# Nine token slots one chunk earlier, the fourth chunk turned on TensorE, three half slots made whole, and one table for the order of all queues

## The chip, the cores and the metric

The kernel runs on one core of a Trainium2 chip. The metric is the device time of one execution in microseconds, median of the runs. Engines: TensorE (PE, matmuls), VectorE (DVE), ScalarE (ACT), GpSimd (POOL, which issues the scatters and the stores) and SyncE (SP, which issues most loads and all turning DMAs).

## The reference

Two stages. A gated linear recurrence runs over 4 sequences of 5056 steps and 256 features, and its output, 20,224 tokens of 256 features, goes through a mixture of 8 experts, where each token takes its best one:

```python
a_t = np.exp(8.0 * sigmoid(r_gate) * log(a_base))
x_gated = np.sqrt(np.maximum(1.0 - a_t * a_t, 1e-06)) * sigmoid(i_gate) * x
h = a_t[:, t] * h + x_gated[:, t]          # for every step t; y[:, t] = h
logits = x @ w_gate                        # x is y, as 20224 x 256
e_idx = np.argmax(logits, axis=1)
h = np.maximum(x[mask] @ w1[e], 0.0)       # 256 -> 1024
out[mask] = gate_w * sigmoid(x @ w_output_gate)[e] * (h @ w2[e])
```

## The kernel before

**Chunks.** The 158 tiles of 128 tokens are worked in 21 chunks: two of four tiles (0 and 1), then chunks of eight, each in blocks of four tiles (512 tokens). Features lie on the partitions, so the recurrence is a scan along the row. For each block `chunk(c)` (L725) loads the gates and x (L752, on SP's queue), makes the gates on ACT (L758, L761, L768, L772, L777) and DVE (L764, L780) and scans on DVE (L812, last column kept by L815). Then the states are *turned*, so that tokens lie on partitions, and *routed*: logits, argmax (L1035 to L1047), a token's rank among those of its expert (matmuls `pk`, L1053 and L1055), its row (L1086 to L1093). GpSimd scatters each tile's rows (L545) to the DRAM array `xs`, which has one region for each expert.

There are two ways of turning. Chunks under `BY_PE` (0 and 1) are turned by TensorE: `project` (L932) multiplies the states, in fp32, by the identity and the two gates, so that turned states and logits come out of PSUM together; ACT writes the high half of the turned states (L948), DVE copies the logits (L951) and writes the low half (L952). All other chunks are split first (ACT the high part, L972; DVE the low part, L979, behind a memset, L977) into `rt`; a turning DMA on SP's queue (L988, the *flip*, one for each block) brings them to `rows_all`, while PE makes the logits from the split states (L996) and DVE sums them (L1004).

**Slots.** `slot(s)` (L1203) runs one expert's network on 128 rows (later 256) of its region. It fetches on SP's queue the address (L1223), the rows by a turning DMA (L1234) and each row's weight and token number (L1235). Layer 1 is L1306 on PE, in two halves of four 128-feature tiles: three f16 products for each weight. ACT takes the relu (L1331, high half), DVE the low half (L1334, `h`), layer 2 is L1381, ACT scales the result (L1402) and GpSimd stores it (L1405). The PSUM tile of layer 1 is free again when its low is done. Slots of the first set are *plain*: they work in fp32 with the weights as loaded (L1276, L1292, L1327, L1367).

`SETS` is the list of fixed slots: a tuple (chunk, first expert, last expert + 1, rows) says that after the counts of this chunk each of these experts has enough rows for one more slot. Each set costs five small DVE operations in `counts` (L1103 to L1112). So slots 0 to 7 need chunk 1, slots 8 to 15 chunk 3, slots 16 to 23 chunk 4, slots 24 to 31 chunk 5. What is left of the rows at the end goes to `ENDS` slots of 128 rows and `HALVES` slots of 64.

**Weights.** `unit(u)` loads one expert's w1 (u even) or w2 (u odd), finds its scale (a gram matrix of it on PE, L627; ACT L633; PE L636; DVE L641, L642) and splits it in two f16 parts (ACT L669, DVE L679). Units 14 and 15, expert 7 of the kernel's numbering, are staged in two pieces each (`fw14_0`, `fw14_1`, `fw15_0`, `fw15_1`) in buffers of the ring `hh`, which the hidden tiles `h` also use.

**The order.** Each step is a `Work` item of an engine or queue. `PLACES` holds a number for each as its rank; `in_order` (L188) runs them through a model of engines and queues and takes of those that are ready in the model the one with the least rank, so that the instructions stand in fixed order on PE, ACT and DVE, and on the DMA queues as they come:

```python
    for w, v in zip(first, places(len(first))):
        w.rank = v
        for w in in_order([w for w in works if not w.late], {"DVE": 1.7, "ACT": 0.8}):
            w.emit()
```

Of the kernel before, what the change touches and what calls it, by code (L numbers as in the profile page):

```python
# [7 lines left out]
F32 = mybir.dt.float32  # L8
# [17 lines left out]
SETS = [(1, 0, 8, 128), (3, 0, 8, 128), (4, 0, 8, 128), (5, 0, 8, 128), (6, 0, 8, 128), (8, 0, 8, 128), (9, 0, 8, 128), (10, 0, 8, 128),  # L26
        (12, 0, 8, 256), (14, 0, 8, 256), (16, 0, 8, 256), (18, 0, 8, 256), (20, 0, 8, 256)]
PROGRAM = "ccwwwwswswswssssws"
PLAIN = (0,)
# [4 lines left out]
BY_PE = 2  # L34
TOP = 6

ENDS = 16
HALVES = 3
# [290 lines left out]
def rglru_moe(ctx: ExitStack, tc: tile.TileContext, x, r_gate, i_gate, a_param, wg, wog, w1, w2, out, shape):  # L329
# [1155 lines left out]
    for w, v in zip(first, places(len(first))):  # L1485
        w.rank = v
# [48 lines left out]
```

## Time and profile before

| what | value |
|---|---|
| runs, median (lowest to highest) | 1009.37 us (1009.24 to 1009.7) |
| the profiled execution, its own time | 1010.89 us |
| its span, first to last instruction | 1009.0 us |
| mean granted TensorE clock | 0.977 |
| PE busy | 940.9 us, 93% of the span |
| DVE busy | 678.2 us, 67% |
| ACT busy | 624.1 us, 62% |
| POOL busy | 359.9 us, 36% |

Busy shares are means over the span. Two phases lie in it: up to about 680 us chunks are scanned and routed beside the slots, and DVE is busy most of the time; after that only slots run, and PE alone is full. The idle time of PE lies in the first quarter. A row of a timeline gives the start, the busy time, the line, the operation, how many instructions it sums up, and in brackets how long the engine had been idle before and what ended that. A start less the next start is what a group costs; busy times of neighbours overlap. A clock of 0.50 is 1.2 GHz, 1.00 is 2.4 GHz.

### The profile page before, as it was taken

To read this page: it belongs to the slowest core of one execution; us is meant where nothing else is said; L and a number is where in the kernel's file an instruction comes from. 1 tells how busy PE (TensorE), PEld (TensorE's weight loads), DVE (VectorE), ACT (ScalarE), POOL (GpSimd) and SP (SyncE) were. 2 spreads that over 40 slices of the span, in tenths; PEclk is the share of its full clock that TensorE was granted. 3 is DMA by queue.
4 is the path that set the end of the run, shared out by engine and by line. 5 is a ranking of instruction groups with operands and counts; after the bars stand their busy time and mean duration, and the time that the engine had idled before them with its cause. 6 is when DMAs were issued, how large, how long until landed. Compare 5 with 4: busy or idle time off the path is not lost.

```text
span 1009.0 us, 27629 instructions
## 1 busy us (share of the span) xinstructions
PE 940.9 (93%) x10796; PEld 860.5 (85%) x10796; DVE 678.2 (67%) x1719; ACT 624.1 (62%) x931; POOL 359.9 (36%) x341
## 2 busy tenths in 40 slices
PE   1389959999999999999999999999999999999996
PEld 1379859998999899999888888988888888899994
DVE  5789998888978898889878987878322222322231
ACT  8799987877777688877778777743322322322321
POOL 2115252544444444445344554444221211221111
PEclk9779988999999999999999999999999999999998
DMA  9999997989999999899988898656522122138771
GB/s 318 338 264 330 241 211 184 218 191 221 212 222 200 209 253 255 166 228 221 249 179 224 203 250 210 122 125 208 113 52 53 48 54 49 47 111 229 247 232 37
DMA packets 269237, 189.75 MB, mean 188 GB/s; under 512 B 211071, under 2 KB 222080, under 8 KB 269104
## 3 DMA queue, kind: packets, MB, share of 16 engines
q1 hardware_dynamic: 249488, 138.37, 59.5%
q0 software_dynamic: 15408, 42.22, 13.7%
q10 hardware_dynamic: 4208, 7.34, 2.0%
q8 instruction: 88, 1.44, 0.6%
q14 instruction: 45, 0.37, 0.1%
HBM read 79.09 MB, written 44.82 MB: 123 GB/s over the span
## 4 chain that ended last, share of the span: by engine, by line
PE 59%; DVE 13%; ACT 11%; DMA 10%; issue 4%; POOL 1%; SPq 1%; ACTq 0%; POOLq 0%; DVEq 0%
PE po L1381 27%; PE ph L1306 27%; DMA out_dram<-ot,osc 3%; DVE it L812 3%; DVE h L1334 3%; DMA it<-in_i_gate_dram 3%; PE po L1367 2%; DVE it L780 2%; ACT it L772 2%; ACT it L777 1%; ACT L777 1%; PE ph L1292 1%; DVE peak L864 1%; DVE xt L764 1%; DMA fw<-in_moe_w_dram 1%
## 5 line engine op out<-in xcount | busy, mean ns | idle before, releaser
L1381 PE MATMUL po<-w2r,h 128*128 128x256 f16 (+2 forms) x3720 | 494.5, 273 | 2.8 <-ACT ot L1402 1.3
L1306 PE MATMUL ph<-xt,w1r 128*128 128x128 f16 (+1 forms) x4608 | 427.1, 241 | 3.9 <-DMA xt<-xs 3.0
L1381 PEld LDWEIGHTS <-h 128*128 128x128 f16 (+1 forms) x3720 | 347.5, 98 | 41.9 <-issue 3.5
L1306 PEld LDWEIGHTS <-w1r 128*128 128x128 f16 x4608 | 349.2, 98 | 30.5 <-DMA xt<-xs 3.4
L1334 DVE SCALAR_TENSOR_TENSOR h<-ph,h 128x512 f16<-128x512 f32 (+1 forms) x310 | 208.3, 680 | 225.6 <-ACT h L1331 222.8
L1331 ACT ACTIVATE h<-ph 128x512 f16<-128x512 f32 (+1 forms) x310 | 180.6, 588 | 253.0 <-PE ph L1306 156.6
L1405 POOL DMA_INDIRECT out_dram<-ot,osc x163 | 174.9, 1073 | 424.7 <-ACT ot L1402 367.0
L545 POOL DMA_INDIRECT xs<-rows_all,posi x158 | 180.0, 1139 | 207.5 <-ACT h L1331 93.9
L1402 ACT ACTIVATE ot<-po,osc 128x256 f32<-128x256 f32 (+1 forms) x163 | 73.2, 469 | 62.2 <-PE po L1381 41.1
L812 DVE TENSOR_TENSOR_SCAN it<-rt,last,it 128x512 f32<-128x512 f32 (+4 forms) x78 | 96.1, 1241 | 0.5
L780 DVE SCALAR_TENSOR_TENSOR it<-it,xt 128x1024 f32<-128x1024 f32 (+1 forms) x40 | 48.3, 1208 | 28.9 <-ACT it L777 28.9
L768 ACT ACTIVATE rt<-rt,lam 128x512 f32<-128x512 f32 (+1 forms) x80 | 62.5, 803 | 2.4 <-issue 1.7
L1306 PE MATMUL ph<-xt,ws 128*128 128x128 f16 (+1 forms) x912 | 63.8, 215 | 0.0
L764 DVE SCALAR_TENSOR_TENSOR xt<-it,xt 128x1024 f32<-128x1024 f32 (+1 forms) x40 | 48.2, 1205 | 18.1 <-ACT it L761 18.1
L1306 PEld LDWEIGHTS <-ws 128*128 128x128 f16 x912 | 55.8, 98 | 4.1 <-issue 2.0
L761 ACT ACTIVATE it<-it 128x1024 f32<-128x1024 f32 (+1 forms) x40 | 41.5, 1040 | 16.1 <-DMA it<-in_i_gate_dram 16.1
L979 DVE SCALAR_TENSOR_TENSOR rt<-it,scale,rt 128x512 f16<-128x512 f32 (+1 forms) x76 | 48.9, 685 | 1.9 <-ACT rt L972 1.8
L772 ACT ACTIVATE it<-rt 128x1024 f32<-128x1024 f32 (+1 forms) x40 | 41.6, 1044 | 10.0 <-DVE xt L764 9.2
L758 ACT ACTIVATE rt<-rt 128x1024 f32<-128x1024 f32 (+1 forms) x40 | 41.7, 1043 | 9.3 <-DMA rt<-in_r_gate_dram 9.0
L777 ACT ACTIVATE it<-it,quarter 128x1024 f32<-128x1024 f32 (+1 forms) x40 | 44.8, 1134 | 0.3
L972 ACT ACTIVATE rt<-it,scale 128x1024 f16<-128x1024 f32 (+1 forms) x38 | 42.0, 1131 | 4.2 <-DVE scale L886 4.1
L864 DVE TENSOR_REDUCE peak<-it 128x1 f32<-128x1024 f32 (+1 forms) x34 | 40.0, 1193 | 0.0
(186 smaller groups left out, 694.1 us busy)
## 6 DMA issues: line engine op xcount, KB each, us to landing
rt<-in_r_gate_dram SPq DMA_DIRECT2D x39, 512.0 KB
it<-in_i_gate_dram SPq DMA_DIRECT2D x39, 512.0 KB
xt<-in_x_dram SPq DMA_DIRECT2D x39, 512.0 KB
ws<-w1r SPq DMA_DIRECT2D x38, 512.0 KB
w1r<-in_moe_w_dram ACTq DMA_DIRECT2D x4, 1024.0 KB
w2r<-in_moe_w_dram SPq DMA_DIRECT2D x4, 1024.0 KB
w2r<-in_moe_w_dram ACTq DMA_DIRECT2D x3, 1024.0 KB
w1r<-in_moe_w_dram SPq DMA_DIRECT2D x3, 1024.0 KB
```

The costliest lines, as they stand in the source:

```text
L545: op = nc.gpsimd.indirect_dma_start(out=xs[:, :], out_offset=bass.IndirectOffsetOnAxis(ap=pos, axis=0), in_=rows.bitcast(F32), in_offset=None,
L768: nc.scalar.activation(r[:, h], r[:, h], AF.Exp, scale=lam[:, h:h + 1], bias=lam[:, h:h + 1])
L772: nc.scalar.activation(t("it"), t("rt"), AF.Square)
L777: nc.scalar.activation(t("it"), t("it"), AF.Sqrt, scale=-0.25, bias=quarter)
L780: nc.vector.scalar_tensor_tensor(t("it"), t("it"), 0.5e-3, t("xt"), op0=ALU.max, op1=ALU.mult)
L812: nc.vector.tensor_tensor_scan(H[:, h, lo:hi], A[:, h, lo:hi], H[:, h, lo:hi], first, op0=ALU.mult, op1=ALU.add)
L1306: nc.tensor.matmul(ph[:, i, 0:w], lhsT=ws[:, f // 2 % 2, a, c, f % 2 * P:(f % 2 + 1) * P], rhs=xt[:, b * ND + c, 0:w], start=n == 0, stop= ...
L1331: newest["relu"] = nc.scalar.activation(part(0, f0), tiles["ph", s, f0][:, :, 0:w], AF.Relu).ins
L1334: nc.vector.scalar_tensor_tensor(part(1, f0), tiles["ph", s, f0][:, :, 0:w], 0.0, part(0, f0), op0=ALU.max, op1=ALU.subtract)
L1381: nc.tensor.matmul(po[0:pw, j], lhsT=hh[:, a, f % 4, j * P:j * P + pw], rhs=second(b), start=f + j + a + b == 0, stop=f == NF - 1 and a == ...
L1402: nc.scalar.activation(ot[0:pw], tiles["po", s][0:pw, j], AF.Copy, scale=tiles["osc", s][0:pw, j, 0:1])
L1405: op = nc.gpsimd.indirect_dma_start(out=out[:, :], out_offset=bass.IndirectOffsetOnAxis(ap=tiles["osc", s][0:pw, j, 1:2].bitcast(I32), axi ...
```

## The change

*Sets.* Experts 0 to 5 get their second slot after chunk 2 and no longer after chunk 3; of the slots that stood after chunk 4, those of experts 3 to 5 stand after chunk 3, beside the second slots of experts 6 and 7. So nine slots stand a chunk earlier. Slots 8 to 13 now need chunk 2, 14 to 18 chunk 3, 19 to 23 chunk 4; from 24 on nothing moves. There are three sets more.

*Turning.* Chunk 3 is turned by PE, like chunks 0 and 1: eight tiles of `project`, no flips, no logit matmuls.

*The end.* Nineteen slots of 128 rows in place of sixteen of 128 and three of 64.

*The order.* `in_order` and its ranks are no longer used for the main part; `ORDER` lists every work item, on all engines and queues, in the order in which it is emitted. `PLAIN` is a dictionary and the plain slots may have another width; both leave the eight plain slots as they are. In the changed file lines stand 5 earlier up to L1420 and 9 earlier near the end.

```diff
@@ -23,19 +23,19 @@
-SETS = [(1, 0, 8, 128), (3, 0, 8, 128), (4, 0, 8, 128), (5, 0, 8, 128), (6, 0, 8, 128), (8, 0, 8, 128), (9, 0, 8, 128), (10, 0, 8, 128),
+SETS = [(1, 0, 8, 128), (2, 0, 6, 128), (3, 6, 8, 128), (3, 3, 6, 128), (4, 0, 3, 128), (4, 6, 8, 128), (5, 0, 8, 128), (6, 0, 8, 128), (8, 0, 8, 128), (9, 0, 8, 128), (10, 0, 8, 128),
         (12, 0, 8, 256), (14, 0, 8, 256), (16, 0, 8, 256), (18, 0, 8, 256), (20, 0, 8, 256)]
...
-PLAIN = (0,)
+PLAIN = {0: 0}
...
-BY_PE = 2
+BY_PE = (0, 1, 3)
...
-ENDS = 16
-HALVES = 3
+ENDS = 19
+HALVES = 0
...
-PLACES = (
...
+ORDER = (
...
-def places(n):
+def laid_out(n):
...
-    return struct.unpack(f"<{n}H", zlib.decompress(base64.b85decode("".join(PLACES))))
+    return itertools.accumulate(struct.unpack(f"<{n}h", zlib.decompress(base64.b85decode("".join(ORDER)))))
...
-        for b in range(0, nt, 4) if c < BY_PE else ():
+        for b in range(0, nt, 4) if c in BY_PE else ():
...
-        if c >= BY_PE:
+        if c not in BY_PE:
             for blk, (pu, pold) in zip(blocks, pus):
...
-        plain = set_of[s] in PLAIN
+        plain = expert is not None and expert >= PLAIN.get(set_of[s], E)
...
-    first = [w for w in works if not w.late]
-    for w, v in zip(first, places(len(first))):
-        w.rank = v
-
     engines = {PE, mybir.EngineType.Activation, mybir.EngineType.DVE}
     with tc.manual_schedule(engines=engines):
-        for w in in_order([w for w in works if not w.late], {"DVE": 1.7, "ACT": 0.8}):
-            w.emit()
+        for k in laid_out(len([w for w in works if not w.late])):
+            works[k].emit()
```

On SP's queue, around the fetch of slot 8 (`xt16_8`) and the pieces of the last weights, before (the rows that only set up a fetch's address are left out):

```order
L752 DMA it_5_4_1509<-in_i_gate_dram 128x2x512
L988 DMA_TRANSPOSE rows_all_134<-rt_4_0_828 128x19x128
L1223 TENSOR_LOAD firsti_1_1325
L1234 DMA_TRANSPOSE xt16_8_1562<-xs_84 128x4x128
L1235 DMA mt_8_1563<-xs_84 128x2
L601 DMA fw15_1_1571<-in_moe_w2_dram 128x4x256
```

and after:

```order
L596 DMA fw14_0_1393<-in_moe_w1_dram 128x1024
L596 DMA fw14_1_1420<-in_moe_w1_dram 128x1024
L1218 TENSOR_LOAD firsti_1_994
L1229 DMA_TRANSPOSE xt16_8_1428<-xs_84 128x4x128
L1230 DMA mt_8_1429<-xs_84 128x2
L596 DMA fw15_0_1487<-in_moe_w2_dram 128x4x256
L596 DMA fw15_1_1531<-in_moe_w2_dram 128x4x256
```

Slot 8's fetch stands ahead of both pieces of `fw15`, and no flip of chunk 4 stands between them (the two flips follow after the fetches of slots 10 and 11).

On DVE, around the low half of slot 8's first hidden tile (`h_8_0`), before:

```order
L679 SCALAR_TENSOR_TENSOR w2r_136<-fw15_0_1476,wsc_137,w2r_136 128x1024
L679 SCALAR_TENSOR_TENSOR w2r_136<-fw15_1_1571,wsc_137,w2r_136 128x1024
L1086 TENSOR_TENSOR pos_4_1748<-pk_4_1712,carry_131 128x64
L1090 TENSOR_TENSOR pos_4_1748<-pos_4_1748,oh_4_1665 128x64
L1093 TENSOR_REDUCE posi_4_1751<-pos_4_1748 128x8
L1062 TENSOR_TENSOR df_4_1622<-oh_4_1665,lz_4_1582 128x64
L1063 TENSOR_REDUCE sm_4_1769<-ex_4_1639 128x8
L1064 TENSOR_REDUCE zs_4_1767<-df_4_1622 128x8
L1334 SCALAR_TENSOR_TENSOR h_8_0_1759<-ph_8_0_1612,h_8_0_1759 128x4x128
L780 SCALAR_TENSOR_TENSOR it_5_4_1509<-it_5_4_1509,xt_5_4_1358 128x1024
L1334 SCALAR_TENSOR_TENSOR h_8_1_1797<-ph_8_4_1632,h_8_1_1797 128x4x128
L1334 SCALAR_TENSOR_TENSOR h_9_0_1810<-ph_9_0_1699,h_9_0_1810 128x4x128
```

and after:

```order
L674 SCALAR_TENSOR_TENSOR w2r_133<-fw15_0_1487,wsc_134,w2r_133 128x1024
L674 SCALAR_TENSOR_TENSOR w2r_133<-fw15_1_1531,wsc_134,w2r_133 128x1024
L999 TENSOR_REDUCE lz_4_1692<-lg_4_0_1515 128x64
L1343 TENSOR_SCALAR osc_7_1702<-mt_7_1278 128x1
L1344 SCALAR_TENSOR_TENSOR osc_7_1702<-again_0_500,mt_7_1278 128x1
L999 TENSOR_REDUCE lz_4_1692<-lg_4_4_1629 128x64
L1030 TENSOR_REDUCE mx_4_1727<-lz_4_1692 128x8
L1031 TENSOR_TENSOR df_4_1729<-lz_4_1692,mx_4_1727 128x64
L1329 SCALAR_TENSOR_TENSOR h_8_0_1694<-ph_8_0_1517,h_8_0_1694 128x4x128
L759 SCALAR_TENSOR_TENSOR xt_5_4_1535<-it_5_4_1625,xt_5_4_1535 128x1024
L1329 SCALAR_TENSOR_TENSOR h_8_1_1741<-ph_8_4_1539,h_8_1_1741 128x4x128
L1329 SCALAR_TENSOR_TENSOR h_9_0_1750<-ph_9_0_1685,h_9_0_1750 128x4x128
```

The positions (`pos_4`, `posi_4`) and the sums (`sm_4`, `zs_4`) of chunk 4 no longer stand ahead of `h_8_0`, and of chunk 5 only the first product (L759) does, where before it was both of these, a scan pair and the first gated input (L775 now, L780 then).

## Rows read from the trace of the kernel before

**Rows 1.** Page part 1: busy time, share of the span, instructions.

```profile
PE 940.9 (93%) x10796; PEld 860.5 (85%) x10796; DVE 678.2 (67%) x1719; ACT 624.1 (62%) x931; POOL 359.9 (36%) x341
```

**Rows 2.** Windows around the hole: stretch, busy us by engine, granted clock, DMA.

```profile
130.00:140.00 10.00, 7.91 (x80) 7.24 (x78) 9.28 (x15) 9.89 (x13) 8.78 (x5) 1.00 0.97 248
140.00:145.00 5.00, 0.82 (x14) 0.61 (x14) 5.00 (x10) 4.66 (x6) 1.33 (x1) 0.82 0.67 157
145.00:155.00 10.00, 5.48 (x35) 4.81 (x36) 6.57 (x14) 5.82 (x9) 1.23 (x1) 0.50 0.90 141
155.00:160.00 5.00, 5.00 (x45) 4.34 (x44) 4.77 (x7) 4.81 (x5) 0.00 (x0) 0.81 1.04 275
```

**Rows 3.** PE's timeline: start, length, line, count, wait before it.

```profile
143.66 0.21 PE L996 MATMUL lg<-g,rt 128*128 128x32 bf16 x1 [3.95 <-DVE rt L979]
...
146.73 1.46 PE L1306 MATMUL ph<-xt,w1r 128*128 128x128 f16 x12 [1.81 <-DMA xt<-xs]
...
151.84 1.03 PE L627 MATMUL pg<-fw 128*128 128x128 bf16 x8 [2.79 <-DMA fw<-in_moe_w_dram]
...
240.47 1.18 PE L1306 MATMUL ph<-xt,w1r 128*128 128x128 f16 x18 [1.16 <-DMA xt<-xs]
```

**Rows 4.** Timeline of SP's DMA queue.

```profile
135.59 5.44 SPq L988 DMA_TRANSPOSE rows_all<-rt  x1
...
146.01 0.37 SPq L601 DMA_DIRECT2D fw<-in_moe_w_dram  x1
```

**Rows 5.** DVE's timeline at slot 8's first low and slot 22's second.

```profile
154.09 0.16 DVE L641 TENSOR_SCALAR wsq<-pg 128x1 int32<-128x1 int32 x1 [3.26 <-PE pg L636]
...
161.22 0.69 DVE L1334 SCALAR_TENSOR_TENSOR h<-ph,h 128x512 f16<-128x512 f32 x1 [0.53 <-ACT h L1331]
...
240.14 0.69 DVE L1334 SCALAR_TENSOR_TENSOR h<-ph,h 128x512 f16<-128x512 f32 x1 [0.46 <-ACT h L1331]
```

**Rows 6.** Windows behind the hole.

```profile
161.20:240.20 79.00, 76.76 (x1088) 71.88 (x1085) 69.21 (x179) 60.74 (x88) 37.41 (x33) 1.00 0.85 199
225.00:250.00 25.00, 22.58 (x320) 21.07 (x317) 21.43 (x59) 16.25 (x24) 11.62 (x10) 1.00 0.97 229
```

**Rows 7.** PE's timeline: starts of like groups in a row.

```profile
31.39 0.71 PE L932 MATMUL lg<-iw,it 128*128 128x144 f32 x4
31.93 0.65 PE L932 MATMUL prow<-iw,it 128*128 128x144 f32 x4
...
182.67 0.26 PE L996 MATMUL lg<-g,rt 128*128 128x48 bf16 x4
182.77 0.49 PE L1381 MATMUL po<-w2r,h 128*128 128x256 f16 x3
...
979.73 0.50 PE L1306 MATMUL ph<-xt,ws 128*128 128x128 f16 x6
980.07 0.49 PE L1381 MATMUL po<-w2r,h 128*128 x3
...
982.07 0.34 PE L1306 MATMUL ph<-xt,ws 128*128 128x64 f16 x6
982.24 0.82 PE L1381 MATMUL po<-w2r,h 128*128 x6
```

**Rows 8.** DVE's groups by line and shape: busy, mean ns of one, idle before.

```profile
L812 DVE TENSOR_TENSOR_SCAN it<-rt,last,it 128x512 f32<-128x512 f32 x70 | 88.6, 1275 | 0.5
L979 DVE SCALAR_TENSOR_TENSOR rt<-it,scale,rt 128x512 f16<-128x512 f32 x74 | 48.1, 691 | 1.9 <-ACT rt L972 1.8
...
L764 DVE SCALAR_TENSOR_TENSOR xt<-it,xt 128x1024 f32<-128x1024 f32 x39 | 47.5, 1218 | 18.1 <-ACT it L761 18.1
...
L952 DVE SCALAR_TENSOR_TENSOR rows_all<-prow,scale,rows_all 128x256 f16<-128x256 f32 x6 | 2.8, 473 | 0.0
...
L1103 DVE SCALAR_TENSOR_TENSOR first<-carry,next_row 128x8 f32<-128x8 f32 x13 | 2.2, 166 | 0.4
...
L951 DVE COPY lz<-prow 128x16 f32<-128x16 f32 x6 | 1.0, 164 | 0.2 <-ACT rows_all L948 0.2
```

More of the change, by code (lines that the diff above doesn't have):

```diff
@@ L744, in load @@
                 bufs = rings[tags[k]].n
-                wide_ = c >= BY_PE and tags[k] == PLANES
+                wide_ = c not in BY_PE and tags[k] == PLANES
                 t = pool.tile(
@@ L886, in level_of_peak @@
             nc.vector.tensor_scalar(sc, sc, float(254 + TOP << 23), None, op0=ALU.add)
[L888 removed]
+        if c not in BY_PE:
             pus = [rings["ps_r"].new() for _ in blocks]
@@ L901, in chunk @@
             en = work("PE", 0.25, energy, [mo], EARLY + c / 100, uses=[pu0], slack=SLACK[c > 4])
-            le = work("DVE", 0.3 + 0.15 * (c >= BY_PE), level, [en], late_rank, uses=[pu0])
+            le = work("DVE", 0.3 + 0.15 * (c not in BY_PE), level, [en], late_rank, uses=[pu0])
         else:
@@ L1038, in chances @@
         def chances():
-            nc.scalar.activation(st("ex", E), st("df", E), AF.Exp, scale=1.0 if c < BY_PE else tiles["inv_of", c])
+            nc.scalar.activation(st("ex", E), st("df", E), AF.Exp, scale=1.0 if c in BY_PE else tiles["inv_of", c])
         def chosen():
@@ L1066, in outer @@
         def outer():
-            nc.scalar.activation(st("zs", 1), st("zs", 1), AF.Exp, scale=-1.0 if c < BY_PE else tiles["inv_of", c])
+            nc.scalar.activation(st("zs", 1), st("zs", 1), AF.Exp, scale=-1.0 if c in BY_PE else tiles["inv_of", c])
         def weights():
@@ L1346, in scales @@
             again = tiles["again", s][0:pw] if expert is None else tiles["again", group][0:pw, place, 0:q]
-            by = tiles["scale", s][0:pw] if expert is None else 1.0 if plain else tab[:, 2, expert:expert + 1]
+            by = tiles["scale", s][0:pw] if expert is None else 1.0 if plain else tab[0:pw, 2, expert:expert + 1]
             nc.vector.tensor_scalar(osc[0:pw, 0:q, 0:1], tiles["mt", s][0:pw, 0:q, 0:1], by, None, op0=ALU.mult)
@@ L1367, in multiply2 @@
                     nc.tensor.matmul(
-                        po[:, 0], lhsT=tiles["hh", s, 0][:, f], rhs=raw_of(2 * expert + 1, f * D, D), start=f == 0, stop=f == NF - 1,
+                        po[0:pw, 0], lhsT=tiles["hh", s, 0][:, f, 0:w], rhs=raw_of(2 * expert + 1, f * D, D), start=f == 0, stop=f == NF - 1,
                     )
```

136 lines of the change are left out of this document (65 added, 71 removed).

## The prediction

> **What bounds the kernel now.** I read the page's busy shares first: TensorE (PE) is busy 93% of the span [rows 1], so the end moves only where PE idles or runs slowly, or where PE is given more or less work. The slices under it say where it idles: the first 175 us, and hardly after. The windows then give the largest hole that is left once the load of inputs is over: between 130 and 160 us PE is busy 7.91 + 0.82 + 5.48 + 5.00 = 19.21 of 30 us, so 10.8 us are idle; and the granted clock falls to 0.82, then 0.50, then 0.81 of full speed [rows 2]. At half the clock 5.48 busy us do 2.74 us of work, and the two windows beside it lose 0.82 × 0.18 + 5.00 × 0.19 = 1.1 us. The hole costs 10.8 + 2.7 + 1.1 = 14.6 us.
>
> What ends PE's waits there [rows 3]: 3.95 us for the last split planes of chunk 4 (L979), 1.81 us for the rows of slot 8 (xt, the first slot after the eight plain ones), 2.79 us for the last quarter of the last expert's weights (fw). The queue on SP shows why the last two are late [rows 4]: the turning DMA of chunk 4 goes out at 135.59 and holds the queue for 5.44 us, and the fetch of slot 8 and the last quarter (146.01) stand behind it. Beneath lies a dearth: the eight plain slots need chunks 0 and 1 alone, and the next slots wait for chunk 3. Nothing else was there for PE.
>
> The second engine is VectorE (DVE): 9.28 of 10 us busy in 130:140, all of 140:145 [rows 2]. It does the low half of every hidden tile (L1334), and PE can't go on without it. Its low of slot 8's first half starts at 161.22, behind waits of 3.26 and 0.53 us [rows 5]. From there to the low of slot 22's second half (240.14), DVE is busy 69.2 of 79 us while PE is busy 76.8 [rows 6]. So PE has the hole, and DVE has a reserve of only some 12% behind it.
>
> **The change, part by part.**
>
> *Work added to PE.* (a) Chunk 3 is turned by projections (L932, four matmuls a tile): the second group of four starts 0.54 us after the first [rows 7]; 8 tiles × 0.54 = 4.3 us more. Its 32 logit matmuls go; four take 0.10 us (182.67 to 182.77) [rows 7], so 0.8 us less. Net +3.5. (b) Three slots of 64 rows become 128 rows. Six layer-1 matmuls of the third product take 0.17 us at 64 columns (982.07 to 982.24) and 0.34 us at 128 (979.73 to 980.07) [rows 7]; each slot has eight such sixes, three slots 24: 24 × 0.165 = +4.0 us. Layer 2 goes by the columns of the weights and stays. From 250 us on PE hardly idles, so all of it shows at the end: **+7.5 us**. The bounds: 4.0 if the projections ran only in time that PE idles anyway, 7.5 if all counts. I take 7.5, since the lead below is counted in work done, the projections among it.
>
> *Work moved on DVE, ahead of slot 8's first low.* The two orders, at the mean prices of [rows 8]: one chunk-5 product L764 and one L780 (1.22 each) and two scans (2.55) move behind it: −5.0. Chunk 3 now needs 8 × (0.16 + 0.47) = 5.0 for the copies and low halves of its projected tiles, in place of four L979 (2.8): +2.2. The choice and positions of chunk 4 go behind, ten small operations of about 0.2: −2.1; other small ones (memsets, sums, copies, of like size) −1.7. Together −6.6 us. The two waits of 3.8 us in front of the low [rows 5] were for the late weights and the relu. The weights' last quarter is now issued ahead of the flips, but it waits for a buffer that DVE's split of the piece before it frees. DVE comes there near 137.4 by my sum. In before, this piece took from 146.01 [rows 4] to 151.84 [rows 3] to reach PE, and from there to DVE's next step at 154.09 [rows 5] 2.25 us more: 137.4 + 5.8 + 2.25 = 145.5, plus about 1 us since its gram now follows slot 8's matmuls, 146.4. DVE would be there at 144.6. So a wait of 1.8 us remains; the bounds are 0 (the piece lands sooner) and 3.3 (as now). Slot 8's low then starts at 161.22 − 6.6 − 3.8 + 1.8 = **152.6 us**, 8.6 us sooner. ScalarE has less to do before it (by the same kind of sum its relu could come at 141), so DVE sets it.
>
> *What DVE pays back.* What went behind has to be done between slot 8 and slot 22: one L764, one L780, two scans (5.0 us), four L979 that come sooner in the new order (2.8), three more sets of counts (five operations of about 0.17, 0.8 a set: 2.5) and small ones (2.1): 12.4 us on top of the 72.0 that DVE needs there now, start to start. With no waiting at all it gets there at 152.6 + 84.4 = **237.0 us**, where before it was 240.14 [rows 5]. Most of what was won at 152 is given back by 237: DVE is the bound over this stretch.
>
> *Where PE stands then.* PE's matmuls counted in each order at their start-to-start distance (the rows of [rows 7] and their like): in the kernel before, PE starts at 240.47, after 1.16 us for slot 23's rows [rows 3], the matmul that has 165.5 us of work ahead of it. In the new order 173.5 us stand ahead of slot 24's layer 1, which that low of slot 22 releases. PE is ahead by (240.47 − 237.0) + (173.5 − 165.5) = 11.5 us. PE idles 2.42 us in 225:250 now [rows 6]; I leave half, 1.2, for waits of the same kind in the new order: 10.3. Then 10.3 − 7.5 = **2.8 us faster**.
>
> *At nothing:* the two flips of chunk 3 that go (SP's queue was not last for PE there), the scatters (GpSimd is busy 8.78 us of 130:140, but 2.6 us of the 20 after [rows 2]), and the wider loads of three slots at the end. ScalarE's eight high halves in place of two long ones lie behind its reserve (60.7 of 79 us busy [rows 6]). If that cover is gone, a flip is worth its 5.44 us of SP's queue [rows 4] and no more, as a gain; the others have no row that prices them apart, and I leave 1 us each way for them in the range.
>
> Against the profiled execution's own time: 1010.89 − 2.8 = 1008.1. The median of the runs stands 1.5 us under it (1009.37), so the forecast is **1006.6 us**.
>
> **The rivals.**
>
> *1. DVE keeps up better.* If the last quarter lands in time (no 1.8) and no waits of the old kind come back (no 1.2), PE is ahead by 10.3 + 1.8 + 1.2 = 13.3: 5.8 faster, 1003.6. If DVE also needs less start to start than I count (2 us in 84), 1001.6. For it: DVE filled 140:145 wholly, 5.00 of 5 us [rows 2]. Against it: over 79 us it never came near that [rows 6].
>
> *2. DVE falls behind, and the end is later than before.* My sum lets DVE work 84.4 us without a single wait. Between 161 and 240 it now waits 79 − 72 = 7 us, mostly for ScalarE's relu. If PE, ScalarE and DVE hand each tile round with a loss, each per cent costs 0.85 us. PE's lead of 10.3 is down to 7.5 at a loss of 3.4%: from there the kernel is slower than before. At 3.4% it is 1009.4 (no change), at 7% 1012.4. For it: of the 10 us of 145:155 DVE works 6.57, since it waits for PE's next tile as PE does for it [rows 2]. Against it: ScalarE, which stands between them, is busy 60.7 of 79 us [rows 6], so tiles should lie ready.
>
> *3. The hole stays.* Slot 8's rows need chunk 2's scatters and counts before the fetch; the fetch still stands behind two weight pieces in SP's queue that wait for buffers of the plain slots. If PE waits until 150 again, the added 7.5 us are all there is: 1016.9. Against it: the fetch is ahead of both flips, and chunk 2 is scattered a whole chunk sooner.
>
> *4. The clock.* Over 150 to 237 PE would wait in small pieces for DVE. The trace shows a granted clock of 0.50 after the idle time of 140:145, and 1.00 over 225:250 with 22.58 of 25 us busy [rows 2, 6]. If the clock fell to 0.50 for one 10 us piece, PE would lose up to 5 us of work: 2.1 slower, 1011.5. The Trainium skill, "TensorE: Matmul & The Clock Gate", section "HAM oscillation — how this bites in real kernels", says that idle gaps of a matmul stream bring the half clock back again and again. By that rule the small waits would have to be long; the row of 225:250 with two waits of over 1 us at full clock speaks against it here.
>
> **How the numbers follow.** The forecast has 0.45, by its own range of 1004 to 1009 (the wait for the last quarter 0 to 3.3, the small waits 0 to 2.4). Rival 1 has 0.18, rival 2 has 0.22, rival 3 has 0.08, rival 4 has 0.07. About 0.2%, 2 us, is what a measurement of this kernel can tell from no change: faster is under 1007.35, slower over 1011.4. Of the forecast 0.34 lies under 1007.35 and 0.11 above. Rival 1 is faster, 0.18. Rival 2 gives 0.02 faster, 0.11 the same, 0.09 slower; rival 3 0.08 slower; rival 4 0.04 the same, 0.03 slower. Faster 0.54, same 0.26, slower 0.20. The range of 8 in 10 reaches from 1001 (rival 1 with the lower DVE price) to 1012 (rival 2 at a loss of 6.5%): about 0.05 lies under it, 0.13 above.
>
> **What would show it.** In the changed kernel's windows 140:145 and 145:155 should be nearly full at a granted clock of 1.00; the first low of slot 8 should start at 150 to 154; DVE should be busy over 85% in 152:237 and end nearly every wait of PE there; slot 22's second low should start at 235 to 240. L932 should be 8 tiles longer by 4 to 5 us, and no row of 64 columns stay at the end. I am wrong if PE still idles over 4 us in 140:155 (rival 3), if slot 22's low comes after 240 (rival 2), or if the clock falls below 1.00 after 160 (rival 4).

## The result: 999.27 us, a ratio of 0.990

The changed kernel takes 999.27 us in the median (995.21 to 1006.96) where the kernel before takes 1009.6 on the same chip: a ratio of 0.990, interval 0.9881 to 0.992. The forecast was 1006.6 with a range down to 1001; the sign was right, the size was not. The profiled execution took 999.0 us, with a span of 997.2.

Page part 1 of the changed kernel, which answers to [rows 1]: PE's share rises to 94%, its busy time by 1.1 us only, and the span is 11.8 us shorter.

```profile
PE 942.0 (94%) x10796; PEld 864.0 (87%) x10796; DVE 684.9 (69%) x1739; ACT 632.1 (63%) x941; POOL 354.8 (36%) x340
```

The windows of [rows 2] in the changed kernel (stretch, busy us of PE, weight loads, DVE, ACT and POOL, granted clock, DMA):

```profile
130.00:140.00 10.00, 7.84 (x91) 6.91 (x90) 9.76 (x18) 9.82 (x13) 2.88 (x4) 1.00 0.91 207
140.00:145.00 5.00, 5.00 (x68) 4.41 (x69) 4.80 (x10) 4.73 (x6) 1.84 (x3) 1.00 0.95 239
145.00:155.00 10.00, 10.00 (x134) 9.25 (x132) 9.65 (x28) 9.80 (x15) 4.29 (x3) 1.00 0.74 151
155.00:160.00 5.00, 3.74 (x55) 3.16 (x54) 4.76 (x16) 3.25 (x6) 1.36 (x2) 1.00 1.30 275
```

PE is full in 140:155 and the clock stays at 1.00 (2.4 GHz); 3.4 of the 30 us are idle, none slow. The hole of 14.6 us is gone.

DVE's timeline at the three places of the forecast: the scale of the last weight quarter, slot 8's first low, slot 22's second low [rows 5].

```profile
139.81 0.15 DVE L636 TENSOR_SCALAR wsq<-pg 128x1 int32<-128x1 int32 x1
...
145.16 0.68 DVE L1329 SCALAR_TENSOR_TENSOR h<-ph,h 128x512 f16<-128x512 f32 x1
...
229.68 1.28 DVE L1329 SCALAR_TENSOR_TENSOR h<-ph,h 128x512 f16<-128x512 f32 x2
```

No wait stands ahead of any of the three. Slot 8's low is at 145.16, where 152.6 was forecast, and slot 22's at 229.68 for 237.0: 7.4 and 7.3 us sooner. The stretch between them is 84.5 us, and the forecast said 84.4. DVE works 80.84 of them (first window below; the second answers to the second of [rows 6]):

```profile
145.20:229.70 84.50, 81.10 (x1153) 75.15 (x1151) 80.84 (x219) 70.58 (x98) 39.12 (x34) 1.00 0.97 225
225.00:250.00 25.00, 24.39 (x357) 22.83 (x355) 22.75 (x63) 18.65 (x29) 11.38 (x12) 1.00 0.97 218
```

**Where the time came from.** For each kernel I sum busy time × granted clock of PE over windows of 2.5 us: the work done so far. Time less this work is PE's *lag* (what it lost by waiting or by a low clock). Both kernels on the chip of the result:

| kernel | lag at 70 us | 130 | 160 | 250 | 700 | last matmul | work in all |
|---|---|---|---|---|---|---|---|
| before | 47.9 | 49.9 | 64.6 | 67.2 | 69.5 | 69.6 | 930.7 |
| after | 41.4 | 43.8 | 47.3 | 50.0 | 54.5 | 54.5 | 934.4 |

Three stretches make the difference. Up to 130 us the changed kernel wins 49.9 − 43.8 = 6.1 us; between 130 and 160 it wins 14.7 − 3.5 = 11.2; behind 160 it loses 7.2 where before loses 5.0, so 2.2 go. It does 3.7 us more work. 6.1 + 11.2 − 2.2 − 3.7 = 11.4, and the spans differ by 11.8; the other 0.4 lies behind the last matmul. The forecast has no term for the first 6.1, all of it won by 70 us. The count of work is good to some 2 us: e2 below, which runs the matmuls of the kernel before in another order, comes to 928.4.

**The start.** In the kernel before, the first routing step (DVE's `oh`, for which PE stands 10.99 us) is late because of ACT. Timelines of ACT and its DMA queue, of DVE and of PE, kernel before:

```profile
36.88 1.06 ACT L761 ACTIVATE it<-it 128x1024 f32<-128x1024 f32 x1 [1.68 <-DMA it<-in_i_gate_dram]
36.89 3.71 ACTq L601 DMA_DIRECT2D w1r<-in_moe_w_dram  x1
40.70 0.47 ACT L948 ACTIVATE rows_all<-lg,scale 128x256 f16<-128x256 f32 x1 [2.76 <-issue]
...
41.21 0.17 DVE L951 COPY lz<-lg 128x16 f32<-128x16 f32 x1 [2.01 <-ACT rows_all L948]
...
44.49 0.21 PE L1053 MATMUL pk<-oh,before 128*128 128x32 f16 x1 [10.99 <-DVE oh L1047]
```

ACT waits for a gate's load, then issues a weight load that holds its queue for 3.71 us, and only then writes the high half of the turned states (L948), for which DVE waits. The same places in the changed kernel:

```profile
34.81 0.45 ACT L943 ACTIVATE rows_all<-lg,scale 128x256 f16<-128x256 f32 x1
...
36.59 0.38 ACTq L596 DMA_DIRECT2D w2r<-in_moe_w_dram  x1
...
35.30 0.17 DVE L946 COPY lz<-lg 128x16 f32<-128x16 f32 x1 [1.85 <-ACT rows_all L943]
...
39.34 0.21 PE L1048 MATMUL pk<-oh,before 128*128 128x32 f16 x1 [3.10 <-DVE oh L1042]
```

The high half is 5.9 us sooner, the weight load behind it holds its queue for 0.38 us, and PE waits 3.10 in place of 10.99. On SP's queue the four small loads of the two gates' weights (`iw`) now go out from 4.50 us, ahead of chunk 2's loads, where before they followed four of these, from 8.23; and ACT's items around the expert weights stand in another order. The forecast's sum takes what stands there as it was. That the one weight load makes PE late is read from these rows; no run moves it alone.

### The profile page after: what moved, and what is told of

It is laid out like the page before. It is cut to its first block, busy times and chain, and to the rows that moved or that the text cites. A ratio compares the mean times of both kernels' runs of the same rounds, so it can differ in the third digit from the quotient of the medians.

```text
span 997.2 us, 27683 instructions
## 1 busy us (share of the span) xinstructions
PE 942.0 (94%) x10796; PEld 864.0 (87%) x10796; DVE 684.9 (69%) x1739; ACT 632.1 (63%) x941; POOL 354.8 (36%) x340
## 4 chain that ended last, share of the span: by engine, by line
PE 74%; DVE 11%; DMA 6%; ACT 4%; issue 3%; SPq 1%; POOL 0%; ACTq 0%; POOLq 0%; DVEq 0%
PE ph L1301 35%; PE po L1376 34%; DVE it L807 2%; DMA it<-in_i_gate_dram 2%; DMA xt<-in_x_dram 2%; DMA out_dram<-ot,osc 2%; PE ph L1287 2%; DVE h L1329 1%; DVE it L775 1%; PE lg L991 1%; DMA xt<-xs 1%; DVE w1r L674 1%; PE po L1362 1%; ACT it L756 1%; DVE w2r L674 1%
## 5 line engine op out<-in xcount | busy, mean ns | idle before, releaser
L1376 PE MATMUL po<-w2r,h 128*128 128x256 f16 (+1 forms) x3720 | 490.2, 272 | 1.6 <-DVE h L1329 1.4
L1376 PEld LDWEIGHTS <-h 128*128 128x128 f16 x3720 | 348.1, 98 | 40.4 <-DVE h L1329 2.4
L1329 DVE SCALAR_TENSOR_TENSOR h<-ph,h 128x512 f16<-128x512 f32 x310 | 210.4, 685 | 222.7 <-ACT h L1326 220.5
L1326 ACT ACTIVATE h<-ph 128x512 f16<-128x512 f32 x310 | 182.2, 592 | 258.1 <-PE ph L1301 187.6
L1400 POOL DMA_INDIRECT out_dram<-ot,osc x163 | 177.5, 1089 | 378.4 <-ACT ot L1397 316.8
L540 POOL DMA_INDIRECT xs<-rows_all,posi x158 | 172.6, 1092 | 248.5 <-ACT h L1326 105.9
L1397 ACT ACTIVATE ot<-po,osc 128x256 f32<-128x256 f32 x163 | 73.4, 468 | 50.9 <-PE po L1376 37.1
L1301 PE MATMUL ph<-xt,ws 128*128 128x128 f16 x912 | 68.9, 219 | 0.0
L1301 PEld LDWEIGHTS <-ws 128*128 128x128 f16 x912 | 60.2, 98 | 2.5
L759 DVE SCALAR_TENSOR_TENSOR xt<-it,xt 128x1024 f32<-128x1024 f32 (+1 forms) x40 | 48.3, 1206 | 14.1 <-ACT it L756 13.0
L775 DVE SCALAR_TENSOR_TENSOR it<-it,xt 128x1024 f32<-128x1024 f32 (+1 forms) x40 | 48.3, 1208 | 11.0 <-ACT it L772 10.9
L967 ACT ACTIVATE rt<-it,scale 128x1024 f16<-128x1024 f32 (+1 forms) x36 | 39.5, 1129 | 2.4 <-DVE scale L881 2.2
```

What stands on the lines that cost most here:

```text
L540: op = nc.gpsimd.indirect_dma_start(out=xs[:, :], out_offset=bass.IndirectOffsetOnAxis(ap=pos, axis=0), in_=rows.bitcast(F32), in_offset=None,
L759: nc.vector.scalar_tensor_tensor(t("xt"), t("it"), 1.0, t("xt"), op0=ALU.add, op1=ALU.mult)
L775: nc.vector.scalar_tensor_tensor(t("it"), t("it"), 0.5e-3, t("xt"), op0=ALU.max, op1=ALU.mult)
L1301: nc.tensor.matmul(ph[:, i, 0:w], lhsT=ws[:, f // 2 % 2, a, c, f % 2 * P:(f % 2 + 1) * P], rhs=xt[:, b * ND + c, 0:w], start=n == 0, stop= ...
L1326: newest["relu"] = nc.scalar.activation(part(0, f0), tiles["ph", s, f0][:, :, 0:w], AF.Relu).ins
L1329: nc.vector.scalar_tensor_tensor(part(1, f0), tiles["ph", s, f0][:, :, 0:w], 0.0, part(0, f0), op0=ALU.max, op1=ALU.subtract)
```

## The experiments

Each kernel is the changed file with other constants and another `ORDER`. Where an experiment undoes a part, the order comes from one of the two kernels, and items that this one doesn't have stand where they stand in the other. They ran on four chips, called B to E here; the chip of the result is called A, and the results don't tell whether A and B are two chips. Every ratio is to the kernel before on the same chip, which takes 1008.84 us on B, 1023.0 on C, 1024.26 on D and 1024.39 on E.

| label | chip | us | ratio [interval] |
|---|---|---|---|
| e1_old_start | B | 1004.71 | 0.9958 [0.993, 0.9986] |
| e2_new_start | B | 1006.98 | 0.9976 [0.9953, 0.9999] |
| e3_whole_ends | B | 1009.76 | 1.002 [0.9998, 1.0041] |
| e4_chunk3_dma | B | 1005.16 | 0.997 [0.9947, 0.9993] |
| e5_chunk3_pe | C | 1033.04 | 1.0081 [1.0047, 1.0114] |
| e6_old_sets | C | 1048.22 | 1.0225 [1.0185, 1.0265] |
| e7_nine_halves | C | 1023.58 | 1.0006 [0.9979, 1.0034] |
| e8_old_sp | C | 1027.15 | 1.0043 [1.0011, 1.0076] |
| after_again | D | 1022.08 | 0.9983 [0.9953, 1.0014] |
| e8_again | D | 1024.82 | 1.0021 [0.9998, 1.0044] |
| e9_old_act | D | 1051.39 | 1.0259 [1.0242, 1.0276] |
| e10_new_sp | D | 1023.57 | 0.9992 [0.9971, 1.0013] |
| after_third | E | 1022.4 | 0.9963 [0.9936, 0.999] |
| e1_again | E | 1029.64 | 1.0055 [1.0026, 1.0084] |
| e8_third | E | 1026.67 | 1.0021 [0.9996, 1.0045] |
| e10_again | E | 1023.63 | 0.9992 [0.9969, 1.0016] |

### The start undone, and the start alone

e1: everything as changed, but the items up to about 70 us in the order of the kernel before. Its first loads on SP:

```diff
-ap, 6 loads (chunks 0, 1), iw x4, 4 loads (chunk 2), zeros, ...
+ap, 10 loads (chunks 0 to 2), iw x4, zeros, ...
```

> The changed kernel with the start of the kernel before: all work items that stood ahead of the first matmul of a slot there (202 of them, on all engines and queues) come first and in that order, the rest follows in the order of the changed kernel. Theory A (the start is a part of the gain of its own: PE stands 6.5 us further at 70 us, and keeps that): about 5 to 6.5 us slower than the changed kernel, 1004 to 1006. Theory B (the nine earlier slots alone made the gain, and the later wait for slot 8 would take up any lead of the start): within 1.5 us of the changed kernel, 998 to 1001.

Measured 0.9958, against 0.990 for the whole change on A: without the new start 4.1 us are won and not 10.3. Windows and lows of e1:

```profile
140.00:145.00 5.00, 3.87 (x51) 3.25 (x50) 4.86 (x12) 5.00 (x10) 1.50 (x2) 1.00 1.29 243
145.00:155.00 10.00, 9.38 (x125) 8.24 (x126) 9.70 (x21) 9.40 (x13) 3.77 (x4) 1.00 0.98 203
```

```profile
151.44 0.68 DVE L1326 SCALAR_TENSOR_TENSOR h<-ph,h 128x512 f16<-128x512 f32 x1
...
236.52 1.28 DVE L1326 SCALAR_TENSOR_TENSOR h<-ph,h 128x512 f16<-128x512 f32 x2
```

The hole is filled all the same, and the lows stand at 151.44 and 236.52. The forecast had 152.6 and 237.0: for a kernel that starts as before does, its sum came out within 1.2 us.

e2: the kernel before, with the new order up to about 70 us.

```diff
-BY_PE = (0, 1, 3)
-ENDS = 19
-HALVES = 0
+BY_PE = (0, 1)
+ENDS = 16
+HALVES = 3
...
+SETS = [(1, 0, 8, 128), (3, 0, 8, 128), (4, 0, 8, 128),
```

> The kernel before (its sets, its turning, its ends), with the 182 items that stand ahead of the first matmul of a slot in the changed kernel put first and in that order; the rest in the order of before. Theory A: VectorE too stands some 5 us further, so all behind it moves, 5 to 6.5 us faster than the kernel before, 1003 to 1005. Theory B: the hole at 130 to 160 us grows by what the start wins, within 1.5 us of the kernel before.

Measured 0.9976, 0.1 to 4.7 us faster, between the two theories. Its lag is 44.1 at 70 us (before 47.9), but 49.0 at 130 (before 49.9) and 62.3 at 160: with nothing new to do before chunk 3, PE waits the lead away. Windows of e2:

```profile
130.00:140.00 10.00, 5.14 (x61) 4.92 (x61) 9.44 (x13) 10.00 (x12) 6.20 (x4) 0.95 0.88 214
140.00:145.00 5.00, 2.92 (x33) 2.56 (x33) 4.90 (x13) 4.05 (x6) 1.23 (x1) 0.50 0.65 157
145.00:155.00 10.00, 7.86 (x50) 6.73 (x51) 6.83 (x10) 6.92 (x9) 0.00 (x0) 0.62 1.07 197
```

So the start's lead lasts only where slots are there to use it: it is worth 6 to 7 us in the changed kernel and some 2 here.

### Which queue makes the start

e8 has the whole change with SP's first loads in the old order, e9 with ACT's first items in the old order, e10 is the kernel before with SP's new order alone.

```diff
-SP: ap, 6 loads, iw x4, 4 loads, zeros, ...
+SP: ap, 10 loads, iw x4, zeros, ...
```

> The changed kernel with the first loads on SP's queue (38 items, up to the first slots) in the order of the kernel before; PE, ScalarE and GpSimd as changed. If the order of the loads makes the faster start: 4 to 6 us slower than the changed kernel, 1003.5 to 1006. If it is the order of ScalarE's work (two roots behind one table load, weight loads issued at other places): under 2 us slower.

> The changed kernel with the first 38 items on SP's queue in the order of the kernel before, everything else as changed, beside the changed kernel on the same chip. If the order of the first loads makes the faster start: 4 to 6 us slower than the changed kernel and PE's lead of some 6 us at 70 us gone. If the order of ScalarE's work makes it: under 2 us slower, lead kept.

e8 came out at 1.0043, and beside the changed kernel on chip D 1024.82 to 1022.08, so 2.7 us are lost. The lag at 70 us is 47.3 and 49.7, where the changed kernel on D has 43.5: the lead of the start is gone whole at 70 us. SP's order is needed. ACT's timeline in e8_third shows what holds the high half there:

```profile
37.90 1.06 ACT L753 ACTIVATE it<-it 128x1024 f32<-128x1024 f32 x1 [4.02 <-DMA it<-in_i_gate_dram]
...
39.57 0.45 ACT L940 ACTIVATE rows_all<-lg,scale 128x256 f16<-128x256 f32 x1
```

No weight load holds ACT's queue long here (0.38 to 0.42 us from 26 to 41 us), but the gate's load lands 5.1 us later than in the changed kernel on the same chip (ACT's step at 37.90 for 32.77).

```diff
-ACT: first items in the order of the changed kernel
+ACT: first items in the order of the kernel before
```

> The changed kernel with ScalarE's first 64 items (its weight loads among them) in the order of the kernel before; SP's queue as changed, PE and VectorE but for some 20 to 40 early items that depend on them as changed. The mirror of the last: 4 to 6 us slower if ScalarE's order makes the faster start, under 2 us slower if SP's loads do.

1.0259, far from both forecasts, with a lag of 56.7 at 70 us. A row of PE's timeline and one of ACT's tell why it can't be read as a price:

```profile
46.44 1.89 PE L619 MATMUL pg<-w2r 128*128 128x128 bf16 x16 [13.06 <-DMA w2r<-in_moe_w_dram]
...
51.28 0.47 ACT L940 ACTIVATE rows_all<-lg,scale 128x256 f16<-128x256 f32 x1 [11.72 <-DVE scale L851]
```

PE's new order asks early for weights that come late when ACT issues its loads in the old order. PE waits 13.06 us, DVE's scale comes behind PE's matmuls, and ACT waits for the scale. It shows that the orders are laid for each other, not what ACT's part is worth.

```diff
-SP: ap, 10 loads, iw x4, zeros, ...
+SP: ap, 6 loads, iw x4, 4 loads, zeros, ...
```

> The kernel before with only the first items on SP's queue (those ahead of the first matmul of a slot) in the order of the changed kernel. If the order of the first loads is worth something by itself: 2 to 6 us faster than the kernel before. If the loads need ScalarE's and VectorE's new order with them: no change or slower.

0.9992: nothing. ACT and its queue in e10:

```profile
34.57 5.37 ACTq L592 DMA_DIRECT2D w1r<-in_moe_w_dram  x1
...
40.03 0.47 ACT L939 ACTIVATE rows_all<-lg,scale 128x256 f16<-128x256 f32 x1 [3.62 <-issue]
```

The weight load's issue now holds ACT's queue for 5.37 us, and the high half comes at 40.03 (before 40.70). So with SP's old order the gate's load holds the start (e8), and with ACT's old order a weight load in ACT's own queue does (e10). The times show that SP's order is needed and isn't enough. That ACT's is the other part is read from these rows; no run separates it from VectorE's and PE's.

### The sets and the turning

e6: the whole change, but with the old sets (slots 8 to 15 need chunk 3 again).

```diff
+SETS = [(1, 0, 8, 128), (3, 0, 8, 128), (4, 0, 8, 128),
```

> The changed kernel with the sets of the kernel before (experts' second slots after chunk 3, third after chunk 4), everything else and the order as changed, except that the items of slots 8 to 10 and 16 to 18 wait in the order until the counts that they need are there. If the nine earlier slots fill the hole: PE idles again for 8 us or more between 125 and 160 us, and the time is 7 to 12 us over the changed kernel, 1006 to 1011. If the order of the queues and the turning of chunk 3 fill it: within 2 us of the changed kernel.

1.0225, in four runs and without the changed kernel beside it; 7 to 12 us over the changed kernel had been expected. Its lag is 43.2 at 70 us, like the changed kernel, and rises from 49.6 to 64.9 between 130 and 160, like before; in one window PE does nothing:

```profile
155.00:160.00 5.00, 0.10 (x2) 0.11 (x3) 0.09 (x2) 1.42 (x2) 0.00 (x0) 0.50 0.65 122
```

It is the nine slots that fill the hole. How far e6 falls behind later is not their price, since its order is made for other slots.

e4: the whole change, with chunk 3 turned by DMA; e5: the kernel before, with chunk 3 turned by PE.

```diff
-BY_PE = (0, 1, 3)
+BY_PE = (0, 1)
```

> The changed kernel with chunk 3 turned by the two DMAs again, its items put where they stood in the kernel before and otherwise the changed order. If the projections only cost PE work: 3.5 us faster than the changed kernel, 996. If they carry a part of the gain, since the flips hold SP's queue ahead of the fetches and chunk 3's rows come later: slower, 2 to 8 us, 1001 to 1007, with PE waiting for rows of slots or for planes between 95 and 160 us.

```diff
-BY_PE = (0, 1)
+BY_PE = (0, 1, 3)
```

> The kernel before with chunk 3 turned by PE and nothing else, its projections put where they stand in the changed order. The forecast's price alone: 3.5 us slower, 1012.5. If the hole takes the projections (PE idles there anyway) and the flips that go let the fetch of slot 8 come sooner: 0 to 4 us faster, 1005 to 1009.

e4 on B is slower than the whole change on A (0.997 to 0.990), though it does less work on PE: 931.1 to 934.4, so the projections cost about 3.3 us (forecast 3.5). It loses its time between 95 and 110 us: its lag at 130 is 53.6, the changed kernel's 43.8. A wait of PE, the wait of ACT behind it, and SP's queue in e4:

```profile
110.60 1.22 PE L1284 MATMUL ph<-xt,w1r 128*128 128x128 f32 x4 [6.63 <-ACT h L1319]
...
106.18 1.06 ACT L753 ACTIVATE it<-it 128x1024 f32<-128x1024 f32 x1 [9.21 <-DMA it<-in_i_gate_dram]
...
95.13 0.63 SPq L744 DMA_DIRECT2D it<-in_i_gate_dram  x1
...
97.39 11.44 SPq L980 DMA_TRANSPOSE rows_all<-rt  x1
```

and the same load in the changed kernel:

```profile
88.12 0.44 SPq L747 DMA_DIRECT2D it<-in_i_gate_dram  x1
```

ACT waits 9.21 us for a gate's load, the eighth of its kind in both kernels. It goes out at 95.13, 7.0 us later than in the changed kernel, where ACT's step stands at 99.25 without a wait; from there to ACT's step it is 11.1 us in both. The flip that holds the queue for 11.44 us is issued behind this load, so it isn't shown to cost anything: e4 pays for the load's place in its order. The forecast costed the flips of chunk 3 at nothing, and that stays open. e5 loses 8 to 10 us on C (1.0081 by ratio), which neither of its two forecasts had. Both have an order that was made for the other way of turning, so what the turning is worth with an order of its own is not settled.

### The half slots

e3: the kernel before, with nineteen whole slots at the end. e7: ten whole and nine half slots, with the count of the last loop set to zero, so that some rows stay without a result.

```diff
-ENDS = 16
-HALVES = 3
+ENDS = 19
+HALVES = 0
```

> The kernel before with nineteen whole slots at the end in place of sixteen whole and three half ones, order as before. The term of the forecast (24 groups of six matmuls at 0.165 us each, all on PE's full stretch) wants +4.0 us, 1013.4. The other reading, that PE's whole busy time rose by 3.7 us only with the projections in it, wants under +1 us.

```diff
-ENDS = 16
-HALVES = 3
+ENDS = 10
+HALVES = 9
...
-            nc.vector.tensor_reduce(tiles["more"], own, axis=AX.X, op=ALU.add)
+            nc.vector.memset(tiles["more"], 0)
```

> The kernel before with ten whole and nine half slots at the end in place of sixteen and three; the count for the loop behind them is set to zero, so rows that find no place in these nineteen slots are left out. By the forecast's reading of the layer-1 rows, a half slot saves 8 x 0.165 = 1.3 us, six more of them 7.9 us: 1001.5. By the rows where half slots stand among themselves (six of layer 1 and three of layer 2 take 0.72 us there and 0.66 us in whole slots) six more cost 6 x 8 x 0.06 = 2.9 us: 1012.

e3 does 930.0 us of work, before 930.7 and e2, on e3's chip, 928.4: making three slots whole costs little or nothing. Its time alone doesn't settle that (1.002, from 0.2 us faster to 4.1 slower). e7 does: six slots halved come out between 2.1 us faster and 3.5 slower, where the forecast's price wants 7.9 faster. PE's timeline shows why. Half slots among themselves, kernel before:

```profile
985.78 0.35 PE L1306 MATMUL ph<-xt,ws 128*128 128x64 f16 x6
986.06 0.52 PE L1381 MATMUL po<-w2r,h 128*64 x3
986.50 0.52 PE L1306 MATMUL ph<-xt,ws 128*128 128x64 f16 x12
```

and whole slots, e3:

```profile
993.07 0.50 PE L1297 MATMUL ph<-xt,ws 128*128 128x128 f16 x6
993.40 0.49 PE L1372 MATMUL po<-w2r,h 128*128 x3
993.73 0.50 PE L1297 MATMUL ph<-xt,ws 128*128 128x128 f16 x6
```

Start to start, six matmuls of layer 1 and three of layer 2 take 0.28 + 0.44 = 0.72 us with 64 rows, and 0.33 + 0.33 = 0.66 with 128. Layer 1 is cheaper with 64, layer 2 dearer; a weight load of layer 2 takes 109 ns with 64 columns and 98 with 128. The pair of [rows 7] (0.17) has a layer 2 of 128 columns of weights behind it: it is where a half slot begins between whole ones.

### The chip

The whole change again on two more chips, and the start once more on one and the same chip with it.

```diff
 (no edit: the changed kernel; e1, e8 and e10 as above)
```

> The changed kernel itself once more, as the measure for the other runs on the same chip: 0.988 to 0.992 of the kernel before.

> The changed kernel once more. On one chip it came out at 0.990 of the kernel before, on another (where the kernel before takes 1024 us) at 0.998. In that second chip's traces TensorE waits 9 to 16 us for nothing that the profile shows ("issue"), in all eight kernels seen there or on a like chip; on the two chips where the kernel before takes 1009 us such waits are 0 in all six. Theory A: the gain hangs on the chip: where PE shows no such waits and the kernel before takes about 1009 us, the ratio is 0.988 to 0.993; where it shows over 8 us of them, 0.996 to 1.001. Theory B: the first ratio was not the kernel's own: then it is 0.995 to 1.000 on a chip without such waits too.

> The changed kernel with the order of the kernel before up to about 70 us. Theory A (the new start gives 5 to 6 us where PE has no waits of the kind above): 0.994 to 0.997 there, and its low of slot 8 some 6 us behind the changed kernel's. On a chip with such waits: the start gives 2 us or less, 0.998 to 1.003. Theory B (start worth nothing of its own, the first comparison was across two chips): within 0.2% of the changed kernel on this same chip.

> The changed kernel with SP's first loads in the order of the kernel before (chunk 2's loads ahead of the gates' weights). It was seen only on chips where PE shows waits for nothing, and lost 2.7 us there against the changed kernel. Theory A (the start needs SP's order): on a chip without such waits 4 to 6 us over the changed kernel, lag of PE at 70 us like the kernel before (47 to 49 us). Rival (ScalarE's order alone makes the start): within 2 us of the changed kernel.

> The kernel before with only SP's first loads in the new order. Theory A (SP's order alone is not enough, since ScalarE's work waits in its old order): 0.997 to 1.002. Rival (SP's order alone makes the start): 0.993 to 0.996 where PE has no waits for nothing.

On E, the changed kernel is 7.2 us ahead of e1 and 4.3 ahead of e8, and e10 gains nothing: the share of the start is real on one and the same chip, and larger than the 2 us that were expected of a chip like E. But the whole change is worth 0.2 to 0.4% on D and E, not 1% (on D, where 0.988 to 0.992 was expected, the interval reaches past 1), and e1 is slower there than before (1.0055). No run repeats the whole change on a chip like A: the 0.990 rests on the one comparison there, and Theory B is not ruled out by a second one. The hole is filled there too: after_third's lag goes from 47.3 to 50.0 between 130 and 160, e10_again's from 51.4 to 65.5. The lead goes afterwards: from 160 to 700 the changed kernel loses 22.1 us on D and 23.7 on E (7.2 on A), kernels with before's sets 12 to 14 (e10; 4.9 before on A). DVE's lows in after_third:

```profile
148.88 0.68 DVE L1329 SCALAR_TENSOR_TENSOR h<-ph,h 128x512 f16<-128x512 f32 x1
...
236.75 0.68 DVE L1329 SCALAR_TENSOR_TENSOR h<-ph,h 128x512 f16<-128x512 f32 x1
```

87.9 us where 84.4 was the sum without a wait; in after_again it is 88.7, in e1_again 89.6. PE's waits in after_third over the whole span, by line and releaser, show what comes with it:

```profile
PE ph L1301 <- issue: 8.6, 17, 1.1
PE ph L1301 <- DVE h L1329: 5.1, 7, 1.9
...
PE pg L622 <- issue: 1.8, 3, 0.8
```

"issue" means that PE waited for nothing the profile shows. Such waits sum to 9 to 16 us in every kernel profiled on C, D and E, and to nothing in all six on A and B. One set of 36 matmuls of layer 1 in after_again, PE's timeline:

```profile
231.70 1.78 PE L1301 MATMUL ph<-xt,w1r 128*128 128x128 f16 x29
234.36 0.27 PE L1301 MATMUL ph<-xt,w1r 128*128 128x128 f16 x2 [0.88 <-issue]
235.85 0.44 PE L1301 MATMUL ph<-xt,w1r 128*128 128x128 f16 x5 [1.22 <-issue]
```

and the window that begins there:

```profile
235.00:240.00 5.00, 4.15 (x44) 3.63 (x45) 2.36 (x4) 1.42 (x3) 0.00 (x0) 0.70 1.12 288
```

The set stops twice in the middle, with its rows and weights long there, and the granted clock falls to 0.70 behind it. Each instruction takes as long as on A (a mean low in 160:500 683 ns on both, a relu 592 and 589, a layer-1 matmul of 128 columns 219 on both): on these chips PE's stream of instructions is held, not the work itself. What holds it is open.

## Why the prediction missed

- *The hole* (14.6 us, filled by the new sets): right. Lag lost in 130:160 is 14.7 before and 3.5 after; with the old sets (e6) it stays.
- *Slot 8's low at 152.6*: this step failed. The sum started from before's own 161.22 and counted what moves ahead of the low; it has no term for the start, which it took as unchanged. The new order wins 6.5 us of lag by 70 us, and the low comes at 145.16. With the old start (e1) it comes at 151.44. The start is worth 10.3 − 4.1 = 6.2 us across chips A and B, and 7.2 on E.
- *The wait of 1.8 us for the last weight quarter*: it did not come, though the account of the buffer was right. SP's queue does wait for DVE's split of the piece before it (first row, from its list of waits: us in all, times, longest), and the quarter goes out when the first half of the split is done. SP, DVE and PE in the changed kernel:

```profile
SPq L596 <- DVE w1r L674: 2.8, 1, 2.8
...
131.37 2.48 DVE L674 SCALAR_TENSOR_TENSOR w1r<-fw,wsc,w1r 128x1024 f16<-128x1024 f32 x2
...
132.98 0.38 SPq L596 DMA_DIRECT2D fw<-in_moe_w_dram  x1
...
134.70 1.22 SPq L1229 DMA_TRANSPOSE xt<-xs  x1
...
138.69 0.38 PE L631 MATMUL pg<-sq,ones 128*128 128x1 f32 x2 [0.29 <-ACT dg L628]
...
140.17 4.70 SPq L983 DMA_TRANSPOSE rows_all<-rt  x1
```

  The flip of chunk 4 stands behind the quarter now [rows 4]. With the old start (e1) DVE begins the split at 137.66, where the sum had 137.4. The size was off: from the split to PE's result the sum took 5.8 + 2.25 + 1 = 9.0 us, and it is 7.7 in both (131.37 to 139.07, 137.66 to 145.35). DVE reaches its next step for this quarter at 139.81, in e1 at 146.09 (the sum had 144.6), when the result is there.
- *DVE pays back 12.4, so that it needs 84.4 us to slot 22*: right, 84.5 measured, 85.1 in e1.
- *PE's work, +7.5 us*: 3.7 measured. The projections are about 3.3 (forecast 3.5). The +4.0 for the half slots is nothing that the runs can tell from zero: the term took layer 1's price at the edge of a half slot and left layer 2 as it was, where layer 2 takes 0.44 us in place of 0.33.
- *Waits behind 160*: 1.2 us were set aside. The changed kernel loses 2.2 us more there than before, e1 5.6 more.
- *Two readings of the trace of before* were off. DVE's waits between 161 and 240 are 8.3 us, and 4.6 of them are for ACT's roots (L777); the relu has 1.8. And slot 8's rows were late not by the flip alone: it ends at 141.03, and SP's queue waits 2.3 us more for scattered rows before the fetch at 144.02.

With the start left as before (e1), the parts are 0.5 + 12.2 − 5.6 − 4.2 = 2.9 us in the profiled execution, and the forecast said 2.8: that is luck, the net of two errors, too much work and too few waits. The missing 6 us are the start.

The rivals: of rival 1 the piece in time came true, the end of the small waits did not; DVE never fell behind on A (rival 2), the hole did not stay (rival 3), the clock stayed at 1.00 from 130 to 250 (rival 4). On D and E, the stretch is as long as rival 2 said: 87.9 to 89.6 us, 4 to 6% over the sum, and the forecast put the point of no gain at 3.4%. With the old start it ends slower than before (e1_again), as the rival said; the new start is what keeps the change ahead there. The cause is not shown to be the rival's: in this stretch of after_third PE waits 3.6 us for nothing that the profile shows, about what the stretch is too long by (3.5).

## What to carry to other kernels

Where a change replaces the order of everything, compare the two orders from the first instruction, and not only around the hole one knows: over half of the gain lay in the first 70 us, which the forecast had not compared. Price a shape from rows of its own kind in a steady stretch, all operations of the step together, and not from the pair at a border. A lead of 1% that a full engine has to hold over hundreds of microseconds can shrink on another chip, so look at a second chip of each kind before it is called a gain.

## What the runs showed of the hardware

- Layer 2 with the hidden tile of 64 rows as the weight (128*64) takes 0.44 us for three matmuls, with 128 rows 0.33; layer 1's six next to it 0.28 with 64 columns and 0.33 with 128. The weight load of 64 columns takes 109 ns, that of 128 columns 98 (kernel before, from 960 us on).
- A weight load issued from ACT's queue stood 3.71 us in ACT's queue and kept ACT idle for 2.76 (5.37 and 3.62 in e10), and took 0.38 us in the changed order.
- The kernel before takes 1009 us on A and B and 1023 to 1024 on C, D and E. In all twelve profiles taken on C, D and E PE stands 9 to 16 us for nothing that the profile shows, and the changed kernel counts 4 to 5 us more work there than on A (938.5 and 939.8 for 934.4).
